# State times weights as 64-column matmuls into the two halves of the output partitions, two tiles per two steps

## The chip, the cores and the metric

The kernel runs on one core of one Trainium2 chip. The metric is the device time of one execution in microseconds (us). A run is timed as a whole; the profile's span, from the first to the last instruction on the core, is a little shorter.

## The reference

`x` is (8, 8, 512, 64): 8 batches, 8 heads, 512 tokens, 64 channels. `state` is (8, 8, 32, 64). Per batch and head:

```
a  = softmax(x @ state.T / 8)   ; xread = a  @ state      (512 x 64)
a2 = softmax(state @ x.T / 8)   ; sread = a2 @ x          ( 32 x 64)
y  = concat of xread and sread over tokens, the heads side by side: (8 * 544, 512)
out = (sigmoid(y @ w_gate) * (y @ w_val)) @ w_out          w_gate, w_val: 512 x 1536, w_out: 1536 x 512
```

## The kernel before

The kernel never forms xread. Since xread of a head is a times that head's state, xread times a weight is a times (state times weight). So for each batch it makes SW, the state of all heads times `w_gate` and `w_val`, and multiplies the attention weights into it. All matmuls are bf16 with fp32 sums in PSUM.

The stationary operand of "state times weight" is `sTz`, filled at L247 to L250. For a pair of heads j it holds 128 columns: the first 64 are the pair's transposed state (head 2j in the upper 64 channel rows, head 2j+1 in the lower, 32 columns each), the last 64 are zeros. `sw_tile(b, t)` (L167 to L179) makes one of the 24 tiles of SW for batch b: 512 columns of one weight (`w` picks gate or value, `q` the third of its columns), and one group `g` of two pairs, whose 2 x 64 rows fill the 128 output partitions. It does so with two matmuls of 128 stationary columns into the whole PSUM tile `swp`, summed up there: the first reads pair 2g with the zeros behind it, so its second 64 output rows get zeros; the second reads the 64 zeros that lie ahead of pair 2g+1, so its first 64 output rows get zeros added. ScalarE then copies the tile to `SW` as bf16 (L179). `swp` has two buffers.

`gv(b, f)` (L182 to L200) makes the gate and the value of 128 of the 1536 columns for 512 tokens: two matmuls each (L192), a tanh on ScalarE (`th`, L199), and a multiply on VectorE (`glu`, L200). `out_mm(b, k)` (L204 to L220) does four matmuls with `w_out` (L209), and every third one is followed by ScalarE's copy of the finished 128x512 tile (`res`, L213) and its DMA; its PSUM pool `p_out` has one buffer, so the next tile's first matmul waits for that copy.

The order is written out by hand in the loop L267 to L310: 12 steps f for each batch b, each with `out_mm` of batch b-1, `gv` of batch b, one `sw_tile` of batch nb = b+1, and then one piece of the attention of batch nb: the transposes of x (`at_xT`, f = 0 and 1), the scores (`at_S`, f = 2 and 3), the normalisation on VectorE (`at_norm`, f = 4 and 5, which makes `ab`), the transposes of `ab` (`at_aT`, f = 6) and sread (`at_sr`, f = 8). In batch 0 the first step of each third of the columns also makes four tiles of SW for batch 0 itself, as the weights arrive by DMA and are cast. In batch 7 there is no next batch, and pass 8 does the sread rows of all batches with plain weights (L195). There is no scheduler: each engine runs its instructions in the order written and waits on semaphores.

Of the kernel before, what the change touches and what calls it, by code (L numbers as in the profile page):

```python
# [16 lines left out]
def kernel(  # L17
# [13 lines left out]
    nc = tc.nc  # L31
# [21 lines left out]
    sTz = wp.tile((128, B, 4, 128), BF, name="sTz")  # L53
# [9 lines left out]
    def load_x(b):  # L63
        xf = stg.tile((128, H, 4, D), FP, name="xf", tag="stg")
        v = x[b].rearrange("h (p c) d -> p h c d", c=4)
        if b == 0:
            for i in range(2):
                nc.sync.dma_start(xf[:, 4 * i:4 * i + 4], v[:, 4 * i:4 * i + 4])
        else:
            nc.sync.dma_start(xf, v)  # L70
        xfs[b] = xf

    def load_w(src, key, q):
        wf = stg.tile((128, 4, 512), FP, name="wf", tag="stg")
        nc.sync.dma_start(wf, src.rearrange("(k p) n -> p k n", p=128)[:, :, q * 512:(q + 1) * 512])
        wfs[key, q] = wf

    def load_wo(q):
        wf = stg.tile((128, 4, 512), FP, name="wof", tag="stg")
        nc.sync.dma_start(wf, moe_w_out.rearrange("(k p) n -> p k n", p=128)[:, 4 * q:4 * q + 4])  # L80
        wfs["o", q] = wf
# [13 lines left out]
    def cast_wo(q):  # L95
        for i in range(4):
            nc.gpsimd.tensor_copy(wo[:, 4 * q + i], wfs["o", q][:, i])


    def at_xT(b, i):  # L100
        if i == 0:
            xTs[b] = ap_.tile((128, 4, 512), BF, name="xT")
        ps = p_at.tile((128, 2, 4, 128), BF, name="xTp", tag="at")
        for jj in range(2):
            for c in range(4):
                j = 2 * i + jj
                nc.tensor.transpose(ps[:, jj, c], xbs[b][:, c, 2 * j:2 * j + 2].rearrange("p h d -> p (h d)"), ident)  # L107
        nc.vector.tensor_copy(xTs[b][:, 2 * i:2 * i + 2], ps.rearrange("p j c t -> p j (c t)"))  # L108

    def at_S(b, i):  # L110
        if i == 0:
            E1s[b] = ap_.tile((128, 4, H * Ns), FP, name="E1")
        ps = p_at.tile((128, 2, H * Ns), FP, name="Sp", tag="at")
        for cc in range(2):
            c = 2 * i + cc
            for j in range(4):
                nc.tensor.matmul(ps[:, cc, j * 64:(j + 1) * 64], xTs[b][:, j, c * 128:(c + 1) * 128],  # L117
                                 sTz[:, b, j, 0:64], start=True, stop=True)
        nc.scalar.activation(E1s[b][:, 2 * i:2 * i + 2], ps, AF.Exp, scale=scale)  # L119

    def at_Eb(b):
        Ebs[b] = ap_.tile((128, 4, H * Ns), BF, name="Eb")
        for c in range(4):
            nc.gpsimd.tensor_copy(Ebs[b][:, c], E1s[b][:, c])  # L124

    def at_norm(b, i):
        if i == 0:
            abs_[b] = ap_.tile((128, 4, H * Ns), BF, name="ab")
        E = E1s[b][:, 2 * i:2 * i + 2].rearrange("p c (h n) -> p (c h) n", n=Ns)
        rs = ap_.tile((128, 16), FP, name="rs")  # L130
        nc.vector.tensor_reduce(rs, E, AX.X, ALU.add)  # L131
        ri = ap_.tile((128, 16), FP, name="ri")
        nc.vector.reciprocal(ri, rs)  # L133
        nc.vector.tensor_tensor(abs_[b][:, 2 * i:2 * i + 2].rearrange("p c (h n) -> p (c h) n", n=Ns), E,  # L134
                                ri.unsqueeze(2).to_broadcast((128, 16, Ns)), ALU.mult)

    def at_aT(b):
        ps = p_at.tile((128, 2, 4, 128), BF, name="aTp", tag="at")
        for g in range(2):
            for c in range(4):  # L140
                nc.tensor.transpose(ps[:, g, c], abs_[b][:, c, g * 128:(g + 1) * 128], ident)  # L141
        aTs[b] = ap_.tile((128, 2, 512), BF, name="aT")
        nc.vector.tensor_copy(aTs[b], ps.rearrange("p g c t -> p g (c t)"))
# [23 lines left out]
    def sw_tile(b, t):  # L167
        if t == 0:
            SWs[b] = fp.tile((128, 2, 2, dff), BF, name="SW", bufs=2)
        q, w, g = t // 4, (t // 2) % 2, t % 2  # L170
        ps = p_sw.tile((128, 512), FP, name="swp")
        W = wg if w == 0 else wv
        for jj in range(2):
            j = 2 * g + jj
            flat = sTz[:, b].rearrange("p j e -> p (j e)")
            lo = j * 128 - 64 * jj
            nc.tensor.matmul(ps, flat[:, lo:lo + 128], W[:, j, q * 512:(q + 1) * 512],  # L177
                             start=(jj == 0), stop=(jj == 1))
        nc.scalar.activation(SWs[b][:, g, w, q * 512:(q + 1) * 512], ps, AF.Copy)  # L179


    def gv(b, f):  # L182
        n = 512 if b < B else B * Ns
        if f == 0:
            glus[b] = fp.tile((128, NF, n), BF, name="glu", bufs=2, padded_shape=(128, NF, 512))
        fs = slice(f * 128, (f + 1) * 128)
        pss = []
        for w in range(2):
            ps = p_gv.tile((128, 512), FP, name="gvp", tag="gv")[:, :n]
            if b < B:  # L190
                for g in range(2):
                    nc.tensor.matmul(ps, SWs[b][:, g, w, fs], aTs[b][:, g], start=(g == 0), stop=(g == 1))  # L192
            else:
                for j in range(4):
                    nc.tensor.matmul(ps, (wg if w == 0 else wv)[:, j, fs], XS[:, j], start=(j == 0), stop=(j == 3))  # L195
            pss.append(ps)
        th = fp.tile((128, 512), FP, name="th")[:, :n]

        nc.scalar.activation(th, pss[0], AF.Tanh, scale=0.5)  # L199
        nc.vector.scalar_tensor_tensor(glus[b][:, f], th, 1.0, pss[1], ALU.add, ALU.mult)  # L200
# [3 lines left out]
    def out_mm(b, k):  # L204
        c, f0 = k // 3, (k % 3) * 4
        if f0 == 0:
            ops[b, c] = p_out.tile((128, 512), FP, name="outp")
        for f in range(f0, f0 + 4):
            nc.tensor.matmul(ops[b, c], glus[b][:, f, c * 128:(c + 1) * 128], wo[:, f],  # L209
                             start=(f == 0), stop=(f == NF - 1))  # L210
        if f0 == 8:
            res = fp.tile((128, 512), FP, name="res")
            nc.scalar.activation(res, ops[b, c], AF.Copy, scale=0.5)  # L213
            if b < B:
                rows = out[b * SC:b * SC + S].rearrange("(p c) n -> c p n", c=4)
                nc.sync.dma_start(rows[c], res)
            else:
                for i in range(4):
                    r0 = (4 * c + i) * SC + S
                    nc.sync.dma_start(out[r0:r0 + Ns], res[i * Ns:(i + 1) * Ns])  # L220
# [20 lines left out]
    for t in range(2):  # L241
        sb = xp.tile((128, H * D), BF, name="sb")
        nc.scalar.activation(sb, sfs[t].rearrange("p h d -> p (h d)"), AF.Copy)  # L243
        ps = p_sw.tile((128, 4, 128), BF, name="stp", tag="swp")
# [22 lines left out]
    for b in range(B + 1):  # L267
        for f in range(NF):
            nb = b + 1 if b + 1 < B else None
            if b == 0:  # L270
                if f % 4 == 0:
                    for t in range(f, f + 4):
                        sw_tile(0, t)
                if f == 1:
                    load_w(moe_w_gate, "g", 2)
                    load_w(moe_w_val, "v", 2)
                if f in (4, 5, 6):
                    load_wo(f - 4)
                if f in (8, 9, 10):
                    cast_wo(f - 8)  # L280
            if b > 0:
                out_mm(b - 1, f)
            gv(b, f)
            if nb is not None:
                sw_tile(nb, f)
                if f == 0:
                    at_xT(nb, 0)
                    if b > 0 and nb + 1 < B:
                        load_x(nb + 1)
                elif f == 1:  # L290
                    at_xT(nb, 1)
                elif f == 2:
                    at_S(nb, 0)
                elif f == 3:
                    at_S(nb, 1)
                elif f == 4:
                    at_norm(nb, 0)
                    at_Eb(nb)
                elif f == 5:
                    at_norm(nb, 1)  # L300
                elif f == 6:
                    at_aT(nb)
                elif f == 8:
                    at_sr(nb)
                if b == 0 and f == 9:
                    load_x(2)
                if nb + 1 < B and f == 11:
                    cast_x(nb + 1, nc.gpsimd, range(4))
            if b == 0 and f in (3, 7):
                cast_w(f // 4 + 1)  # L310
# [32 lines left out]
```

## Time and profile before

| | |
|---|---|
| median of 3 runs | 294.54 us (294.14 to 294.59) |
| the profiled execution's own time | 292.45 us |
| its span | 290.7 us |
| TensorE (PE) busy | 254.0 us, 87% of the span |
| ScalarE (ACT) busy | 152.8 us, 53% |
| VectorE (DVE) busy | 131.7 us, 45% |
| mean granted TensorE clock | 0.998 of 2.4 GHz |

PE is the matrix engine's matmul stream and PEld its weight loads, which lie beside it. A matmul's row has a modelled end, and its duration includes a tail that the next matmul overlaps. So a stream's pace is read from the starts of successive groups, not from durations.

### The profile page before, as it was taken

The page shows a single profiled execution, that of the slowest core. Times are in us where ns is not written, and L with a number is a line of the kernel's source. Part 1 is how long each engine was busy: PE and PEld are TensorE (multiplying, and loading weights), DVE is VectorE, ACT ScalarE, POOL GpSimd, SP SyncE. Part 2 cuts the span into 40 slices and gives each one's busy share as a digit, 9 for nine tenths or more (in the row PEclk, how much of TensorE's full clock was granted, in tenths as well). Part 3 has the DMA queues.
Part 4 walks back from the last instruction along what each step waited for, and adds up shares of the span by engine and source line. Part 5 has one row for each costly group of instructions (what it writes and reads, how often), then busy time and mean ns, then how long its engine had stood idle before and what let it go on. Part 6 is the DMA issues. An engine that isn't in the chain of part 4 may idle for free.

```text
span 290.7 us, 4172 instructions
## 1 busy us (share of the span) xinstructions
PE 254.0 (87%) x1600; PEld 130.8 (45%) x1600; DVE 131.7 (45%) x216; ACT 152.8 (53%) x264; POOL 37.4 (13%) x78
## 2 busy tenths in 40 slices
PE   0044688599999999999999999999999999999993
PEld 0034243245454545454545454545454544456651
DVE  3026364654554455445544554455445543342210
ACT  0333378675755575557555655565566554432330
POOL 0006016800500050005000500050002000000000
PEclk9999999999999999999999999999999999999999
DMA  7977706900110611061105101511101001011102
GB/s 229 338 241 270 293 2 227 341 12 6 53 41 29 177 54 38 28 178 53 39 26 182 48 37 33 183 39 36 38 36 39 36 36 39 36 72 38 72 37 72
DMA packets 20276, 27.53 MB, mean 95 GB/s; under 512 B 3104, under 2 KB 11296, under 8 KB 20256
## 3 DMA queue, kind: packets, MB, share of 16 engines
q1 hardware_dynamic: 18080, 26.74, 27.1%
q10 hardware_dynamic: 2176, 0.52, 0.9%
q8 instruction: 12, 0.20, 0.3%
q14 instruction: 8, 0.07, 0.1%
HBM read 18.35 MB, written 8.91 MB: 94 GB/s over the span
## 4 chain that ended last, share of the span: by engine, by line
PE 77%; DVE 10%; DMA 5%; ACT 4%; issue 1%; ACTq 0%; DVEq 0%
PE outp L209 28%; PE gvp L192 25%; PE swp L177 12%; DMA sf<-in_state_dram 5%; PE gvp L195 4%; PE xTp L107 3%; DVE glu L200 3%; DVE rs L131 3%; DVE ab L134 2%; PE aTp L141 2%; PE srp L157 1%; PE srp L152 1%; ACT wv L93 1%; PE Sp L117 1%; DVE ri L133 1%
## 5 line engine op out<-in xcount | busy, mean ns | idle before, releaser
L200 DVE SCALAR_TENSOR_TENSOR glu<-th,gvp 128x512 bf16<-128x512 f32 (+1 forms) x108 | 70.9, 657 | 124.4 <-ACT th L199 107.4
L209 PE MATMUL outp<-wo,glu 128*128 128x512 bf16 x408 | 104.1, 379 | 0.7 <-ACT res L213 0.7
L192 PE MATMUL gvp<-aT,SW 128*128 128x512 bf16 x384 | 99.7, 382 | 0.1
L199 ACT ACTIVATE th<-gvp 128x512 f32<-128x512 f32 (+1 forms) x108 | 61.7, 572 | 65.5 <-PE gvp L192 55.1
L179 ACT ACTIVATE SW<-swp 128x512 bf16<-128x512 f32 x96 | 56.9, 597 | 30.3 <-PE swp L177 30.3
L192 PEld LDWEIGHTS <-SW 128*128 128x128 bf16 x384 | 37.5, 98 | 45.6 <-ACT SW L179 1.6
L209 PEld LDWEIGHTS <-glu 128*128 128x128 bf16 x408 | 37.9, 98 | 38.0 <-issue 1.0
L124 POOL CAST Eb<-E 128x256 bf16<-128x256 f32 x32 | 13.0, 435 | 179.8 <-ACT E L119 179.8
L177 PE MATMUL swp<-wg,sTz 128*128 128x512 bf16 x96 | 28.9, 389 | 6.4 <-DVE wg L92 6.4
L177 PEld LDWEIGHTS <-sTz 128*128 128x128 bf16 x192 | 19.0, 100 | 31.2 <-issue 6.9
L213 ACT ACTIVATE res<-outp 128x512 f32<-128x512 f32 x34 | 20.3, 597 | 21.0 <-PE outp L209 21.0
L177 PE MATMUL swp<-wv,sTz 128*128 128x512 bf16 x96 | 29.0, 389 | 0.7 <-ACT SW L179 0.7
L108 DVE COPY xT<-xTp 128x1024 bf16<-128x1024 bf16 x16 | 11.1, 691 | 13.8 <-PE xTp L107 13.7
L89 POOL CAST xb<-xf 128x512 bf16<-128x512 f32 x28 | 16.8, 642 | 0.8 <-DMA xf<-in_x_dram 0.8
L246 PE MATMUL stp<-ident,sb 128*128 128x128 bf16 x8 | 1.2, 306 | 16.4 <-ACT sb L243 16.4
L134 DVE TENSOR_TENSOR ab<-E,ri 128x512 bf16<-128x512 f32 x16 | 12.6, 785 | 0.6
L141 PE MATMUL aTp<-ident,ab 128*128 128x128 bf16 x64 | 6.6, 231 | 5.9 <-DVE ab L134 5.2
L107 PE MATMUL xTp<-ident,xb 128*128 128x128 bf16 x128 | 10.6, 230 | 1.1 <-DVE xb L89 1.1
L131 DVE TENSOR_REDUCE rs<-E 128x16 f32<-128x512 f32 x16 | 10.8, 676 | 1.2 <-ACT E L119 1.2
L107 PEld LDWEIGHTS <-xb 128*128 128x128 bf16 x128 | 9.1, 103 | 4.7 <-DVE xb L89 1.4
L119 ACT ACTIVATE E<-Sp 128x512 f32<-128x512 f32 x16 | 9.4, 592 | 3.1 <-PE Sp L117 3.1
L160 DVE RECIPROCAL r<-srp 128x128 f32<-128x128 f32 x8 | 7.7, 957 | 4.0 <-PE srp L157 4.0
(31 smaller groups left out, 102.6 us busy)
## 6 DMA issues: line engine op xcount, KB each, us to landing
out_dram<-res SPq DMA_DIRECT2D x32, 256.0 KB, 2.2
xf<-in_x_dram SPq DMA_DIRECT2D x7, 1024.0 KB, 7.2
wf<-in_moe_w_gate_dram SPq DMA_DIRECT2D x3, 1024.0 KB, 8.3
wf<-in_moe_w_val_dram SPq DMA_DIRECT2D x3, 1024.0 KB, 5.3
wof<-in_moe_w_out_dram SPq DMA_DIRECT2D x3, 1024.0 KB, 5.0
xf<-in_x_dram SPq DMA_DIRECT2D x2, 512.0 KB, 4.8
sf<-in_state_dram ACTq DMA_DIRECT2D x8, 64.0 KB, 8.0
out_dram<-res SPq DMA_DIRECT2D x8, 64.0 KB, 1.7
```

What stands on the lines that cost most here:

```text
L89: eng.tensor_copy(xb.rearrange("p c h d -> p h c d")[:, 2 * i:2 * i + 2], xf[:, 2 * i:2 * i + 2])
L107: nc.tensor.transpose(ps[:, jj, c], xbs[b][:, c, 2 * j:2 * j + 2].rearrange("p h d -> p (h d)"), ident)
L124: nc.gpsimd.tensor_copy(Ebs[b][:, c], E1s[b][:, c])
L131: nc.vector.tensor_reduce(rs, E, AX.X, ALU.add)
L134: nc.vector.tensor_tensor(abs_[b][:, 2 * i:2 * i + 2].rearrange("p c (h n) -> p (c h) n", n=Ns), E, ri.unsqueeze(2).to_broadcast((128, 16, ...
L177: nc.tensor.matmul(ps, flat[:, lo:lo + 128], W[:, j, q * 512:(q + 1) * 512], start=(jj == 0), stop=(jj == 1))
L179: nc.scalar.activation(SWs[b][:, g, w, q * 512:(q + 1) * 512], ps, AF.Copy)
L192: nc.tensor.matmul(ps, SWs[b][:, g, w, fs], aTs[b][:, g], start=(g == 0), stop=(g == 1))
L199: nc.scalar.activation(th, pss[0], AF.Tanh, scale=0.5)
L200: nc.vector.scalar_tensor_tensor(glus[b][:, f], th, 1.0, pss[1], ALU.add, ALU.mult)
L209: nc.tensor.matmul(ops[b, c], glus[b][:, f, c * 128:(c + 1) * 128], wo[:, f], start=(f == 0), stop=(f == NF - 1))
L213: nc.scalar.activation(res, ops[b, c], AF.Copy, scale=0.5)
```

## The change

`sw_tile` no longer pads. Each pair of heads is one matmul with 64 stationary columns, `sTz[:, b, j, 0:64]`, that writes only its own 64 output partitions, and each is a sum of its own. The number of matmuls stays two for each tile, and each still streams 512 columns. In the loop, the tile of an odd step is made in the even step before it, right behind that step's own, so that SW matmuls come four at a time in every second step. The functions around `sw_tile` are unchanged; the lines between it and the loop move up by two (L192 becomes L190).

```diff
         for jj in range(2):
             j = 2 * g + jj
-            flat = sTz[:, b].rearrange("p j e -> p (j e)")
-            lo = j * 128 - 64 * jj
-            nc.tensor.matmul(ps, flat[:, lo:lo + 128], W[:, j, q * 512:(q + 1) * 512],
-                             start=(jj == 0), stop=(jj == 1))
+            nc.tensor.matmul(ps[jj * 64:(jj + 1) * 64], sTz[:, b, j, 0:64], W[:, j, q * 512:(q + 1) * 512],
+                             start=True, stop=True)
         nc.scalar.activation(SWs[b][:, g, w, q * 512:(q + 1) * 512], ps, AF.Copy)
...
             if nb is not None:
-                sw_tile(nb, f)
+                if f % 2 == 0:
+                    sw_tile(nb, f)
+                    sw_tile(nb, f + 1)
                 if f == 0:
```

In the built program each 64-column matmul and its weight load carry the half of the array's columns that they use, the lower for the first pair of a tile and the upper for the second; all 1408 others carry the whole 128 x 128 array. The 192 matmuls of SW stand in 45 groups between the others: 42 of four, and three of eight (batch 0's own tiles).

TensorE before, in batch 1 behind the gate and value matmuls of step f = 4 (`gvp` is their PSUM tile, `sTz` and `glu` name stationary operands):

```order
L192 MATMUL gvp_715<-aT_456,SW_278 128x512
L177 LDWEIGHTS sTz_86
L177 MATMUL swp_721<-wg_87,sTz_86 128x512
L177 LDWEIGHTS sTz_86
L177 MATMUL swp_721<-wg_87,sTz_86 128x512
L209 LDWEIGHTS glu_268
L209 MATMUL outp_680<-wo_89,glu_268 128x512
```

TensorE at the same place in the changed program:

```order
L190 MATMUL gvp_715<-aT_460,SW_278 128x512
L175 LDWEIGHTS sTz_86
L175 MATMUL swp_721<-wg_87,sTz_86 64x512
L175 LDWEIGHTS sTz_86
L175 MATMUL swp_721<-wg_87,sTz_86 64x512
L175 LDWEIGHTS sTz_86
L175 MATMUL swp_725<-wg_87,sTz_86 64x512
L175 LDWEIGHTS sTz_86
L175 MATMUL swp_725<-wg_87,sTz_86 64x512
L207 LDWEIGHTS glu_268
L207 MATMUL outp_684<-wo_89,glu_268 128x512
```

Four half-width matmuls in two PSUM tiles stand where two full-width ones in one tile stood, and step f = 5 has none.

ScalarE before, in batch 1 from the tanh of step 4 on (`res` is the copy that frees the one PSUM buffer of `out_mm`):

```order
L199 ACTIVATE th_718<-gvp_712 128x512
L179 ACTIVATE SW_604<-swp_721 128x512
L213 ACTIVATE res_740<-outp_680 128x512
L199 ACTIVATE th_749<-gvp_743 128x512
L179 ACTIVATE SW_604<-swp_752 128x512
```

ScalarE at the same place in the changed program:

```order
L197 ACTIVATE th_718<-gvp_712 128x512
L177 ACTIVATE SW_604<-swp_721 128x512
L177 ACTIVATE SW_604<-swp_725 128x512
L211 ACTIVATE res_744<-outp_684 128x512
L197 ACTIVATE th_753<-gvp_747 128x512
```

The copy `res` of the odd steps 5 and 11 stands behind two copies of SW instead of one, and the tanh of the odd step follows it.

## Rows read from the trace of the kernel before

**Rows 1.** The page: the span, 40 slices of PE and its clock, chain, weight loads.
```profile
span 290.7 us, 4172 instructions
...
PE   0044688599999999999999999999999999999993
...
PEclk9999999999999999999999999999999999999999
...
PE 77%; DVE 10%; DMA 5%; ACT 4%; issue 1%; ACTq 0%; DVEq 0%
...
L177 PEld LDWEIGHTS <-sTz 128*128 128x128 bf16 x192 | 19.0, 100 | 31.2 <-issue 6.9
```
**Rows 2.** Busy time by stretch: start, batch 0, batches 1 to 6 (span, then engines).
```profile
0.00:41.80 41.80, 17.13 (x126) 10.39 (x127) 15.18 (x27) 14.06 (x21) 5.32 (x14) 1.00 0.71 239
41.80:64.82 23.02, 17.14 (x108) 7.84 (x106) 13.04 (x20) 17.74 (x29) 12.01 (x20) 1.00 0.54 183
64.82:239.12 174.30, 173.57 (x1110) 87.20 (x1109) 90.15 (x145) 104.14 (x181) 20.09 (x44) 1.00 0.19 61
```
**Rows 3.** Timeline of PE, last step of batch 2, first of batch 3: start, us.
```profile
120.54 1.03 PE L209 MATMUL outp<-wo,glu 128*128 128x512 bf16 x4
121.40 1.03 PE L192 MATMUL gvp<-aT,SW 128*128 128x512 bf16 x4
122.27 0.59 PE L177 MATMUL swp<-wv,sTz 128*128 128x512 bf16 x2
122.70 1.03 PE L209 MATMUL outp<-wo,glu 128*128 128x512 bf16 x4
123.56 1.03 PE L192 MATMUL gvp<-aT,SW 128*128 128x512 bf16 x4
124.42 0.59 PE L177 MATMUL swp<-wg,sTz 128*128 128x512 bf16 x2
124.86 0.61 PE L107 MATMUL xTp<-ident,xb 128*128 128x128 bf16 x8
125.30 1.03 PE L209 MATMUL outp<-wo,glu 128*128 128x512 bf16 x4
```
**Rows 4.** Groups of PE by form: busy us, mean ns of one, idle before.
```profile
L209 PE MATMUL outp<-wo,glu 128*128 128x512 bf16 x408 | 104.1, 379 | 0.7 <-ACT res L213 0.7
```
**Rows 5.** Timeline of PE around the transposes of ab in one batch.
```profile
139.58 0.51 PE L141 MATMUL aTp<-ident,ab 128*128 128x128 bf16 x6
...
139.93 0.38 PE L209 MATMUL outp<-wo,glu 128*128 128x512 bf16 x1
```
**Rows 6.** Timeline of all engines, the same batch, from the tanh of step 4.
```profile
133.55 1.03 PE L192 MATMUL gvp<-aT,SW 128*128 128x512 bf16 x4
...
134.81 0.69 DVE L200 SCALAR_TENSOR_TENSOR glu<-th,gvp 128x512 bf16<-128x512 f32 x1 [1.71 <-ACT th L199]
...
138.84 0.69 DVE L134 TENSOR_TENSOR ab<-E,ri 128x512 bf16<-128x512 f32 x1
...
139.16 0.93 PE L141 MATMUL aTp<-ident,ab 128*128 128x128 bf16 x8
```
**Rows 7.** Waits in 64.82 to 239.12 us: total, times, longest.
```profile
PEld L141 <- DVE ab L134: 1.6, 5, 0.3
```
**Rows 8.** Timeline of ACT at the end of batch 2.
```profile
120.74 0.60 ACT L179 ACTIVATE SW<-swp 128x512 bf16<-128x512 f32 x1 [0.27 <-PE swp L177]
121.60 0.60 ACT L213 ACTIVATE res<-outp 128x512 f32<-128x512 f32 x1 [0.27 <-PE outp L209]
```
**Rows 9.** Timeline of PE in the last third of batch 0.
```profile
56.30 1.04 PE L177 MATMUL swp<-wg,sTz 128*128 128x512 bf16 x4 [1.69 <-DVE wg L92]
57.59 1.08 PE L177 MATMUL swp<-wv,sTz 128*128 128x512 bf16 x4 [0.25 <-ACT SW L179]
...
62.23 1.03 PE L192 MATMUL gvp<-aT,SW 128*128 128x512 bf16 x4
63.09 0.59 PE L177 MATMUL swp<-wv,sTz 128*128 128x512 bf16 x2
63.52 1.03 PE L192 MATMUL gvp<-aT,SW 128*128 128x512 bf16 x4
```
**Rows 10.** Timeline of ACT over the same group of four tiles.
```profile
56.95 1.08 ACT L179 ACTIVATE SW<-swp 128x512 bf16<-128x512 f32 x2
58.22 1.08 ACT L179 ACTIVATE SW<-swp 128x512 bf16<-128x512 f32 x2 [0.19 <-PE swp L177]
```

## The prediction

> **What bounds the kernel now.** I read the slices of the page first: from the ninth slice to the last but one PE stands at 9 of 10, at the full clock of 2.4 GHz, and the chain of waits lies on PE for 77% of the span [rows 1]. Then the stretches: in batches 1 to 6, 174.30 us long, PE is busy for 173.57 us, while ACT has 104 us and DVE 90 us of work; in batch 0 PE has 17 us of 23 and ACT 17.7 us [rows 2]. So a change on PE is worth its full size in batches 1 to 6 and little before. Last the pace. In the timeline of PE four matmuls of 512 columns take 121.40 - 120.54 = 0.864 us and the two of an SW tile 122.70 - 122.27 = 0.432 us: 0.216 us each, with no gap between groups, whatever the operands [rows 3]. One matmul's row is 0.379 us long [rows 4], so a tail of 0.163 us lies beside its successor. Weight loads of 0.100 us each for SW [rows 1] lie beside running matmuls as well, and eight transposes follow each other in 125.30 - 124.86 = 0.44 us, 0.055 us each, a new weight load for each [rows 3].
>
> **The change part by part.** The number of matmuls, their columns and the copies to SW stay. What is new is that a matmul holds half of the array's columns and writes half of the partitions, and that its partner has the other half: other weights, another right-hand side, other output rows.
>
> *1. Two halves at once.* No row of this trace has two matmuls in two parts of the array, so the price of a pair is bounded: from above by two in turn, 0.432 us; from below by one behind which the second starts as soon as its weights are in, 0.216 + 0.055 = 0.271 us. I take the lower end, since the two share neither columns nor outputs, and since loading weights beside a running matmul is what the rows show all the time. A group of four (two pairs) then holds PE for 0.432 + 0.055 = 0.487 us, where its four matmuls took 0.864 us: 0.377 us gained. There are 6 x 6 = 36 such groups in batches 1 to 6: 13.6 us.
>
> The Trainium skill speaks for the lower end ("TensorE: Matmul & The Clock Gate", section "Measured speedup vs the span model"): three matmuls in separate column strips ran 2.38 times as fast as in turn. No run here shows it yet; by the other bound of the pair part 1 would be worth nothing.
>
> *2. The switches.* Each group is entered from full-width matmuls and left to them. What one such switch costs (call it s) no row shows. From below: nothing, as transposes, scores and 512-column matmuls follow each other without a gap [rows 3]. From above: if the array has to be empty first, the tail of 0.163 us and then a weight load that could not run ahead, 0.100 us [rows 1], together 0.26 us. The nearest row is PE's restart after the wait for `ab`: six transposes from 139.58 to 139.93, 0.35 us against 6 x 0.055 = 0.33 us [rows 5], so a late weight load itself cost about 0.02 us there, and an empty array would cost 0.18 us. Whether the array has to be empty is open, so I take the middle of the two bounds, s = 0.13 us. Per group 2 x 0.13 = 0.26 us is given back, and 0.117 us is left; over 36 groups 4.2 us. The group pays for itself up to s = 0.19 us.
>
> *3. The transposes of `ab`.* From the tanh of step 4 VectorE works without a pause, from 134.81 until `ab` is done at 138.84 + 0.69 = 139.53 [rows 6], and PE waits 0.3 us for it in the middle of the transposes, five times [rows 7]. The work of VectorE does not change. On PE, between the first half of step 4's `gv` and the transposes, stand 24 matmuls now, 24 x 0.216 = 5.19 us; after the change two, a group of four, sixteen, a group of four: 18 x 0.216 + 2 x 0.487 + 4s = 4.86 + 4s. At s = 0.13 that is 5.38 us, 0.19 us more slack, so the waits shrink from 0.3 to 0.1 us: 5 x 0.19 = 0.9 us gained. At s = 0 they grow by 0.33 us in each of six batches, 2.0 us; at 0.26 they are gone, 1.6 us gained.
>
> *4. ScalarE behind a pair of tiles.* Copies of SW now come two in a row, and in steps 5 and 11 the copy `res`, on which the next `out_mm` waits for its only PSUM buffer, stands behind both. From the rows a copy starts about 0.42 us after its last matmul starts and lasts 0.60 us, and `res` starts 0.20 us after PE leaves `out_mm` [rows 3, 8]. Counted from the first half-width matmul: the two copies run from 0.475 to 1.675 us, `res` could start at 0.487 + s + 0.864 + 0.20 = 1.55 + s, and PE asks for the buffer at 0.487 + s + 1.728 = 2.215 + s. With `res` from 1.68 to 2.28 us and 0.05 us to signal, PE waits 0.11 - s: nothing at s = 0.13, and at s = 0 twelve times 0.11, 1.3 us. A tanh behind the copies has over 1.2 us until its buffer is needed. The tile that is made a step earlier is used only in the next batch, its PSUM buffer is the other of two, and the next group comes over 3.9 us later. No DMA, no instruction of POOL or VectorE moves.
>
> *5. Batch 0.* The three groups of eight wait for weights and then go at ScalarE's pace: four copies from 56.95 to 59.30 us, 0.59 us each, against 0.43 us of PE for a tile [rows 9, 10], so neither a faster pair nor a switch shows: 0. The six groups of four stand in steps of 63.52 - 62.23 = 1.29 us on PE against two copies, 1.18 us, on ScalarE [rows 9, 10]: two steps can gain 0.2 us at most, and at s = 0.26 they lose 0.14 us each. I take 0, with bounds of 0.5 us gained and 0.9 us lost. Batch 7 and pass 8 have no SW.
>
> **Sum.** -4.2 (parts 1 and 2) - 0.9 (part 3) + 0 + 0 = -5.1 us. The profiled execution, 292.45 us (290.7 in the span and 1.75 around it), becomes 287.3 us. It lies 2.1 us under the median of the runs shown; against that median of 294.54 us the forecast is **289.4 us**. At s = 0 with the full gain it is -13.6 + 2.0 + 1.3 = -10.3 us, 284.2 us, and 1 or 2 us less if the second half starts at once and batch 0 gives its bit.
>
> **Rivals.**
>
> *The array must be empty at every switch.* Then s is 0.18 to 0.26 us, and from 0.19 us on the group loses: at 0.26 us 36 x 0.143 = 5.1 us, and 0.9 us in batch 0, less the 1.6 us of the vanished waits: +4.4 us, 298.9 us. It decides from s = 0.21 us on, where 42 groups x (0.42 - 0.377) = 1.8 us outweigh the 1.6 us of the vanished waits. For it speaks that the restart row prices it at 0.18 us even with a cheap weight load; against it that no change of shape in the rows opens a gap. The Trainium skill states this rule ("TensorEngine Tiling (Array Packing)", section "Key Properties"): changing the tiling mode drains the engine. The trace before has one mode only and can't agree or disagree.
>
> *The halves run one after the other* (the change does not do what it is for). Then nothing is gained and only switches are paid: 42 groups x 2s less the vanished waits. At s = 0.13 that is 42 x 0.26 - 1.6 = +9.3 us, 303.9 us; at 0.05 it is about +3.5 us, 298 us; at s = 0 no change. For it speaks that no row shows two matmuls at once, against it that they share no column.
>
> *The overlap is full and switches are nearly free.* Then VectorE's `ab` and ScalarE's `res` are what PE waits for next, and the time is the 284.2 us worked out above.
>
> **How the numbers follow.** About 0.2% of the median, 0.6 us, is what a measurement can tell from no change. The halves overlap and s is under 0.20: 0.58, of which the free switch is about 0.18; this is "faster", and its own range is 282.5 to 293.5 us. They overlap and s is above 0.21: 0.17. They run in turn and switches cost: 0.15, so "slower" is 0.32. The narrow strip around s = 0.21, or halves in turn with free switches, makes "same" 0.10. The range for 8 in 10 takes in both ends of s with overlap, 283 to 299, and the cheaper part of the third case, up to 301 us.
>
> **What would show it.** In the profile after, the two matmuls of a pair should start about 0.06 us apart, and from the point where the full-width stream would go on to the next full-width matmul a group of four should take 0.487 + 0.26 = 0.75 us, where four took 0.864. A start 0.216 us after its partner's shows halves in turn; 0.9 us or more for a group shows the empty array. PE's wait for `ab` should fall to about 0.1 us, with no wait for `res` in batches 1 to 6. A granted clock below 1.00 in batches 1 to 6, or a wait of PE for `swp`, would make the sum wrong in a way that it does not count.

## The result and the profile after

The changed kernel takes 286.36 us (median of 4 runs, 285.03 to 287.04) against 294.48 us: a ratio of 0.9721, interval 0.9685 to 0.9757. A second series gave 286.36 us and 0.9732 (0.9700 to 0.9765). That is 8.1 us faster, where 5.1 us were forecast, inside the stated range. The profiled execution is one at the median: 286.36 us, span 284.6 us. The profiled execution of before was 2 us faster than its median, so the two spans differ by 6.1 us only.

The page after, with the lines that answer to [rows 1]:

```profile
span 284.6 us, 4172 instructions
...
PE   0034596499999999999999999999999999999993
...
PEclk9999997979999999999999999999999999999999
...
PE 77%; DVE 10%; DMA 5%; ACT 4%; issue 2%; ACTq 0%
...
L175 PEld LDWEIGHTS <-sTz 128*64 128x64 bf16 x192 | 7.9, 112 | 30.7 <-issue 25.3
```

PE bounds the kernel as before. What is new is the clock's line: in the seventh and the ninth slice, both in batch 0, the granted clock is below 1.00.

Busy time by stretch, answering to [rows 2]: start, batch 0, batches 1 to 6 up to the same matmul of batch 7 (span, then PE, PEld, DVE, ACT, POOL, clock, DMA share, GB/s).

```profile
0.00:41.65 41.65, 16.62 (x129) 9.77 (x130) 15.10 (x27) 14.06 (x22) 5.33 (x14) 1.00 0.74 240
41.65:65.89 24.24, 17.10 (x106) 6.30 (x105) 13.25 (x20) 17.58 (x29) 12.34 (x20) 0.86 0.51 174
65.89:233.03 167.14, 166.26 (x1110) 75.21 (x1109) 88.90 (x145) 100.91 (x182) 20.17 (x44) 1.00 0.19 62
```

Batches 1 to 6 lost 174.30 - 167.14 = 7.2 us. Batch 0 ended 1.1 us later, at a mean clock of 0.86. The timeline of PE in the changed kernel, answering to [rows 3]:

```profile
122.18 1.03 PE L190 MATMUL gvp<-aT,SW 128*128 128x512 bf16 x4
123.13 0.62 PE L175 MATMUL swp<-wg,sTz 128*64 128x512 bf16 x4
123.69 0.62 PE L107 MATMUL xTp<-ident,xb 128*128 128x128 bf16 x8
124.14 1.03 PE L207 MATMUL outp<-wo,glu 128*128 128x512 bf16 x4
```

The four `gv` matmuls from 122.18 on hold PE for 0.864 us, to 123.04. The group of four starts at 123.13, so the switch in costs 0.09 us, and the next full-width matmul starts at 123.69: from 123.04 the group held PE for 0.65 us, where its four matmuls took 0.864. All 36 groups of batches 1 to 6 hold it for 0.65 us. A closer look inside the group (the first two matmuls alone, and the weight loads):

```profile
123.13 0.41 PE L175 MATMUL swp<-wg,sTz 128*64 128x512 bf16 x2
```
```profile
123.13 0.14 PEld L175 LDWEIGHTS <-sTz 128*64 128x64 bf16 x4 [0.42 <-issue]
```

The rows of the first two matmuls last 0.403 us each and the two together 0.41 us, so both start within 0.01 us of each other: the halves run at once. All four weight loads lie in the group's first 0.14 us, none ahead of it. The Trainium skill ("TensorE: Matmul & The Clock Gate", section "Measured speedup vs the span model") gives about 4 ns from one packed matmul to the next, and the trace agrees within that hundredth.

### The profile page after: what moved, and what is told of

It is laid out like the page before. It is cut to its first block, busy times and chain, and to the rows that moved or that the text cites. A ratio compares the mean times of both kernels' runs of the same rounds, so it can differ in the third digit from the quotient of the medians.

```text
span 284.6 us, 4172 instructions
## 1 busy us (share of the span) xinstructions
PE 246.2 (87%) x1600; PEld 116.6 (41%) x1600; DVE 130.8 (46%) x216; ACT 149.4 (53%) x264; POOL 37.8 (13%) x78
## 4 chain that ended last, share of the span: by engine, by line
PE 77%; DVE 10%; DMA 5%; ACT 4%; issue 2%; ACTq 0%
PE outp L207 30%; PE gvp L190 25%; PE swp L175 9%; DMA sf<-in_state_dram 5%; PE gvp L193 4%; PE xTp L107 3%; DVE glu L198 2%; DVE ab L134 2%; DVE rs L131 2%; ACT th L197 2%; PE srp L152 2%; PE aTp L141 2%; PE Sp L117 2%; PE srp L157 1%; DVE wg L92 1%
## 5 line engine op out<-in xcount | busy, mean ns | idle before, releaser
L190 PE MATMUL gvp<-aT,SW 128*128 128x512 bf16 x384 | 100.5, 385 | 0.1
L177 ACT ACTIVATE SW<-swp 128x512 bf16<-128x512 f32 x96 | 52.1, 594 | 17.5 <-PE swp L175 16.1
L190 PEld LDWEIGHTS <-SW 128*128 128x128 bf16 x384 | 37.2, 99 | 46.2 <-issue 2.5
L207 PEld LDWEIGHTS <-glu 128*128 128x128 bf16 x408 | 37.0, 98 | 40.1 <-issue 5.9
L175 PE MATMUL swp<-wg,sTz 128*64 128x512 bf16 x96 | 16.5, 427 | 7.6 <-DVE wg L92 7.6
L175 PEld LDWEIGHTS <-sTz 128*64 128x64 bf16 x192 | 7.9, 112 | 30.7 <-issue 25.3
L108 DVE COPY xT<-xTp 128x1024 bf16<-128x1024 bf16 x16 | 11.0, 688 | 15.4 <-PE xTp L107 15.4
L175 PE MATMUL swp<-wv,sTz 128*64 128x512 bf16 x96 | 16.5, 418 | 1.0 <-ACT SW L177 1.0
L134 DVE TENSOR_TENSOR ab<-E,ri 128x512 bf16<-128x512 f32 x16 | 11.6, 727 | 0.6
```

The lines of the kernel that those rows point to most:

```text
L175: nc.tensor.matmul(ps[jj * 64:(jj + 1) * 64], sTz[:, b, j, 0:64], W[:, j, q * 512:(q + 1) * 512], start=True, stop=True)
```

## The experiments

**Two halves at once, or something else in the edit?** The edit does three things together: narrower weight loads, two halves of the array, and groups of two tiles. The first three runs take them apart.

*One tile in every step, halves as in the change.*

```diff
-                if f % 2 == 0:
-                    sw_tile(nb, f)
-                    sw_tile(nb, f + 1)
+                sw_tile(nb, f)
```

> Halves as in the change, but one tile in every step: 12 groups of two matmuls in a batch where the change has 6 of four. If the gain is two halves at once, less about 0.19 us for the two switches of a group (0.085 us in, 0.10 us out in the profile after), a group of two holds PE for 0.216 + 0.03 + 0.19 = 0.43 us, what two full-width matmuls held it for: batches 1 to 6 take 173 us as before, and the time is 293 to 295 us. If the gain came from narrower weight loads or from the padding that is gone, it does not depend on the grouping, and the time stays at 286 us.

Measured: 292.72 us, ratio 0.9968 (0.9935 to 1.0002). Its timeline of PE:

```profile
117.50 0.59 PE L190 MATMUL gvp<-aT,SW 128*128 128x512 bf16 x2
118.03 0.41 PE L175 MATMUL swp<-wg,sTz 128*64 128x512 bf16 x2
118.36 1.04 PE L207 MATMUL outp<-wo,glu 128*128 128x512 bf16 x4
119.24 0.59 PE L190 MATMUL gvp<-aT,SW 128*128 128x512 bf16 x2
```

From 117.50 + 0.432 = 117.93, where the full-width stream ends, to 118.36 a group of two holds PE for 0.43 us, as two full-width matmuls did. The two switches eat the overlap, as expected (the time came out just under the 293 to 295 us forecast): from batch 1's first matmul to batch 7's PE needs 173.6 us, before it was 173.4 and in the change 166.3. The gain depends on the grouping, so narrow weight loads or the missing padding alone do not bring it.

*The grouping alone, with the padded full-width matmuls of before.*

```diff
-                sw_tile(nb, f)
+                if f % 2 == 0:
+                    sw_tile(nb, f)
+                    sw_tile(nb, f + 1)
```

> Full-width padded matmuls as before, but two tiles in every second step: the grouping alone. Halves at once: no gain, 294 to 295 us, batches 1 to 6 at 173 to 175 us. If the grouping brings the gain, by fewer waits between PE and ScalarE: 286 to 288 us. Its batch 0 tells whether the 1.1 us that batch 0 lost come with the grouping (it ends 1 us late here too) or with the halves (it ends as before, near 64.8 us, at a granted clock of 1.00).

Measured: 293.53 us, ratio 0.9992 (0.9962 to 1.0022): the grouping alone brings nothing that can be told from no change. In its profiled execution batch 0 ended at 66.6 us, 1.8 us late, with padded matmuls throughout. So batch 0 can end late without the halves. Whether the grouping makes it late is taken up below.

*Both matmuls of a tile in the lower half.*

```diff
-            nc.tensor.matmul(ps[jj * 64:(jj + 1) * 64], sTz[:, b, j, 0:64], ...
+            nc.tensor.matmul(ps[0:64], sTz[:, b, j, 0:64], ...
-        nc.scalar.activation(SWs[b][:, g, w, q * 512:(q + 1) * 512], ps, AF.Copy)
+        nc.scalar.activation(SWs[b][0:64, g, w, q * 512:(q + 1) * 512], ps[0:64], AF.Copy)
```

> The change with both 64-column matmuls of a tile in the lower half of the columns and of the output partitions; the upper half of SW is set to zero by POOL, so half of the heads are left out. Same number of matmuls, same narrow weight loads, same grouping and switches, but no second half to run beside. If the gain is two at once, a group takes four matmuls in turn, 4 x 0.216 + 0.19 = 1.05 us instead of 0.65: 36 x 0.40 = 14 us more than the change, about 300 us, 6 us slower than before. If the gain lies in the narrow loads, 286 us.

Measured: 304.60 us, ratio 1.039 (1.0336 to 1.0444). Its timeline of PE:

```profile
118.14 1.05 PE L176 MATMUL swp<-wv,sTz 128*64 128x512 bf16 x4
119.12 0.62 PE L141 MATMUL aTp<-ident,ab 128*128 128x128 bf16 x8
```

The same four narrow matmuls with the same narrow loads now take 0.98 us from their start instead of 0.56, about what four in turn would. From the start of batch 1 to the matmul behind the last group this kernel needs 178.0 us and the change 164.5: 13.5 us, the 14 us expected. By the groups alone it would be 15.4 us: from the end of the full-width stream each holds PE for 1.08 us instead of 0.65, 36 times. The other 1.9 us come back because the transposes of `ab` no longer wait here as they do in the change: the eight in the last line above take 0.46 us to the next matmul, in the change 0.78. The whole time is 4 to 5 us above the 300 us expected because batch 0 was late as well, by 5.5 us more than in the change; its own memsets on POOL and its longer groups lie there, and it was not taken apart. The gain is shown to be the overlap of two halves.

**Does the order in the queue matter?** The two lower halves of a group first, then the two upper ones (the two tiles' copies follow both):

```diff
+        pss = [p_sw.tile((128, 512), FP, name="swp") for _ in range(2)]
+        for jj in range(2):
+            for g in range(2):
+                j = 2 * g + jj
+                nc.tensor.matmul(pss[g][jj * 64:(jj + 1) * 64], sTz[:, b, j, 0:64], W[:, j, q * 512:(q + 1) * 512],
+                                 start=True, stop=True)
```

> The change with one thing else: within a group the two tiles' lower halves are issued first, then the two upper halves, so that neighbours in the queue want the same half. If matmuls start in the order of the queue and two run at once only when neighbours want different halves, a group takes one matmul more, 0.216 us x 36 = 7.8 us: 294 us. If a matmul may start before its turn when its half is free, or if the gain is not the overlap at all: 286 us.

Measured: 286.53 us, ratio 0.974 (0.9687 to 0.9792), as the change. The first expectation is wrong. The group of this kernel:

```profile
120.06 0.41 PE L189 MATMUL swp<-wv,sTz 128*64 128x512 bf16 x2
```
```profile
120.06 0.62 PE L189 MATMUL swp<-wv,sTz 128*64 128x512 bf16 x4
```

Two start together and four take 0.62 us, as in the change, though the second in the queue wants the same half as the first. With the run before, where matmuls of one half went in turn, this means that an upper half's matmul starts ahead of a lower half's that stands in front of it. The semaphores in the trace's single records say the same: a lower half's matmul waits for its PSUM tile and an upper half's signals that the tile is done, and in all 36 groups the four start in the order waits, signals, waits, signals, where the queue has waits, waits, signals, signals. Matmuls are not started strictly in the order of the queue across halves.

**Batch 0 and the clock.** In the changed kernel batch 0 by stretches of the granted clock, and its longest wait:

```profile
44.40:47.80 3.40, 2.95 (x10) 0.90 (x11) 0.13 (x1) 2.55 (x5) 2.63 (x5) 0.50 0.45 152
47.80:58.00 10.20, 5.91 (x35) 2.09 (x34) 7.75 (x12) 6.86 (x11) 6.57 (x11) 1.00 1.02 347
58.00:61.50 3.50, 3.46 (x12) 0.87 (x11) 0.40 (x1) 2.16 (x4) 1.04 (x2) 0.51 0.12 41
```
```profile
44.59 1.06 PE L175 MATMUL swp<-wg,sTz 128*64 128x512 bf16 x4 [2.54 <-DVE wg L92]
```

Twice the clock is at 1.2 GHz for 3.4 us; ahead of the first, PE had stood idle for 2.54 us, waiting for cast weights, and in the stretch ahead of the second it was busy for 5.9 us of 10.2. The first trial put batch 0 back to what it was:

```diff
+            if full:
+                flat = sTz[:, b].rearrange("p j e -> p (j e)")
+                lo = j * 128 - 64 * jj
+                nc.tensor.matmul(ps, flat[:, lo:lo + 128], W[:, j, q * 512:(q + 1) * 512],
+                                 start=(jj == 0), stop=(jj == 1))
+                continue
...
-                        sw_tile(0, t)
+                        sw_tile(0, t, True)
...
+                if b == 0:
+                    sw_tile(nb, f, True)
-                if f % 2 == 0:
+                elif f % 2 == 0:
```

> Batch 0 with full-width matmuls, one tile in each step, as before; halves in groups of four from batch 1 on. If the halves and their grouping cost batch 0 its 1.1 us, by longer idle of PE after which the granted clock falls to 1.2 GHz for a while, then batch 0 ends near 64.8 us again with the clock at 1.00, batches 1 to 6 take 166 us, and the time is 1 to 1.5 us under that of the change, 285 us. If batch 0's millimetres come from the DMA of that run alone, no difference, 286 us.

(The last sentence of the expectation speaks of batch 0's 1.1 us.) Measured: 287.03 us, ratio 0.9765 (0.9726 to 0.9805), no better than the change. Its batch 0 ended at 67.4 us although its instructions are those of before. Its stretches show 10.2 us at 1.2 GHz, where the profiled execution of before had none [rows 2]:

```profile
44.80:48.20 3.40, 3.27 (x8) 1.10 (x8) 0.00 (x0) 2.27 (x5) 1.44 (x3) 0.51 0.84 302
48.20:55.10 6.90, 4.71 (x27) 2.23 (x27) 6.29 (x10) 3.23 (x7) 5.55 (x9) 0.99 1.01 346
55.10:61.90 6.80, 5.32 (x13) 1.52 (x12) 1.95 (x2) 5.07 (x8) 3.21 (x4) 0.50 0.33 108
```

The expectation falls: batch 0 ends late, and the clock falls in it, without the edit too. The same batch 0 gets a fallen clock in one execution and none in another. Nor does every fall show in the time: the run with one tile in every step had 3.4 us at 1.2 GHz too, from 57.0 to 60.4 us, and ended batch 0 at 64.8 us like before. Over whole executions time and clock go together: in one series of 23 of the kernel before, those with a mean clock of 0.997 or 0.998 took 291.9 to 293.1 us, those at 0.985 or below 294.3 to 295.5 us. The next trial goes for the idle time itself, eight extra matmuls ahead of the second and the third group of batch 0's own tiles:

```diff
+            nc.tensor.matmul(dum[0], ones[:, 0], wg[:, 0, 0:512], start=True, stop=True)
...
+                    if f > 0:
+                        keep_busy(8)
```

> The change with eight extra full-width matmuls (1.7 us, into a PSUM tile that nobody reads) ahead of the second and third group of batch 0's own tiles, where PE waits for weights 2.5 and 2.1 us. If the granted clock falls in batch 0 because PE sits idle there, it stays at 1.00 up to batch 7 in most executions, batch 0 ends 1 to 2 us earlier, and the time is 284.5 to 285.5 us with less spread. If the clock has other reasons, or costs nothing because ScalarE sets the pace there, 286 to 287 us.

Measured: 284.18 us (283.22 to 284.81), ratio 0.9682 (0.9649 to 0.9715), with mean clocks of 0.991 to 1.00, where the change itself had 0.979 to 0.992 in its ten executions, in other series. Batch 0 ended at 64.3 us in the profiled execution, though that one still had one stretch of 3.4 us at 1.2 GHz:

```profile
51.86 0.51 PE L141 MATMUL aTp<-ident,ab 128*128 128x128 bf16 x6 [1.76 <-DVE ab L134]
52.21 1.62 PE L190 MATMUL gvp<-aT,SW 128*128 128x512 bf16 x4
53.62 3.03 PE L227 MATMUL outp<-wg,ones 128*128 128x512 bf16 x8
```

The wait for `ab`, 1.76 us, was not filled, and the clock fell behind it (the eight extra matmuls then took 3.0 us instead of 1.7). The next two versions, which were timed beside this one, have no extra matmuls in batch 0: their mean clocks were 0.982 to 0.994, so the higher clock goes with the filling. But their profiled executions ended batch 0 at 64.1 and 63.7 us, as early as this one, and the interval of the ratio overlaps that of the change (0.9685 to 0.9757). So that the filling makes batch 0 shorter is not shown. Whether the edit makes a fall likelier than before is not settled either: the kernel before was also seen at 0.983.

**More from fewer switches.** Groups of three tiles need a third PSUM buffer for SW, which the attention's pool gives up:

```diff
-    p_sw = ctx.enter_context(tc.tile_pool(name="p_sw", bufs=2, ...
-    p_at = ctx.enter_context(tc.tile_pool(name="p_at", bufs=2, ...
+    p_sw = ctx.enter_context(tc.tile_pool(name="p_sw", bufs=3, ...
+    p_at = ctx.enter_context(tc.tile_pool(name="p_at", bufs=1, ...
...
+                k = 2 if b == 0 else 3
+                if f % k == 0:
+                    for t in range(f, f + k):
+                        sw_tile(nb, t)
```

> The change with groups of three tiles (six matmuls) in every third step from batch 1 on: four groups a batch instead of six. It takes a third PSUM buffer for SW from the attention's pool, which keeps one. If a group's fixed price is 0.19 us of switches, and each further pair 0.216 us, a group of three takes 0.19 + 0.03 + 3 x 0.216 = 0.87 us, where twelve tiles took 6 x 0.65 = 3.9 us and now take 4 x 0.87 = 3.5: 6 x 0.4 = 2.5 us gained, 284 us. But only one group stands between step 4 and the transposes of ab, so PE's wait for VectorE there grows by about 0.4 us in each batch and gives the gain back: 286 us. A start stage that grows by the single attention buffer would show ahead of batch 0.

Measured: 284.06 us, ratio 0.9694 (0.9654 to 0.9734); from batch 1's first matmul to batch 7's it needs 165.4 us, 0.9 us less than the change. Most of the rest of the 2.5 us went where it was expected, into the wait for `ab`, as its table of waits in batches 1 to 6 shows:

```profile
PEld L141 <- DVE ab L134: 3.7, 6, 0.6
PE aTp L141 <- DVE ab L134: 2.7, 6, 0.5
```

The weight loads of these transposes waited 3.7 us here and 1.9 us in the change (its row stands further below). The time is nevertheless at the 284 us of the full gain, because batch 0 ended at 64.1 us in the profiled execution, 1.8 us ahead of the change; the start stage did not grow, and why batch 0 was shorter was not taken apart. So the transposes of `ab` were moved one step later:

```diff
-                elif f == 6:
+                elif f == 7:
                     at_aT(nb)
```

> As the groups of three, with the transposes of ab one step later (step 7), so that VectorE has about 1.7 us more. If the wait for ab is what gives the gain back, it is gone now, its 0.3 us of before too: 6 x 0.7 = 4 us under the groups of three alone, 282 to 283 us. If PE waits somewhere else (for res or a PSUM buffer), less.

Measured: 279.54 us (279.13 to 279.72), ratio 0.9533 (0.9503 to 0.9564). The expectation had 4 us under the groups of three alone, and it is 4.5; the 282 to 283 us it gave were counted from 286. In batches 1 to 6 no wait of PE or of its weight loads names `ab` any more, and from batch 1's first matmul to batch 7's it needs 161.6 us, 4.7 us less than in the change and 11.8 us less than before. A group of three in its timeline, with the four `gv` matmuls ahead of it:

```profile
118.45 1.03 PE L190 MATMUL gvp<-aT,SW 128*128 128x512 bf16 x4
119.41 0.62 PE L175 MATMUL swp<-wg,sTz 128*64 128x512 bf16 x4
119.87 0.38 PE L175 MATMUL swp<-wv,sTz 128*64 128x512 bf16 x2
120.18 0.62 PE L107 MATMUL xTp<-ident,xb 128*128 128x128 bf16 x8
```

Six matmuls hold PE from 118.45 + 0.864 = 119.31 to 120.18: 0.87 us, as worked out, where six in turn take 1.296. Then both gains together, with no further edit:

> Groups of three tiles, the transposes of ab in step 7, and the eight extra matmuls twice in batch 0. If the two gains lie in different stretches (batches 1 to 6: 4.6 us against the change; batch 0: about 1.5 us) they add: 1 to 2 us under the groups of three with the later transposes, 0.947 to 0.950 of before. If batch 0's gain is lost to the wait for ab's transposes or to the clock falling elsewhere, 0.953 as without it.

Measured: 278.89 us (277.62 to 279.44), ratio 0.9475 (0.9439 to 0.9511), clocks of 0.997 to 0.999 in all six executions. Batches 1 to 6 again need 161.6 us, and batch 0 ended at 63.2 us with no fall of the clock. It is the fastest version here by its median, 5% under before and 2.6% under the change, which was timed beside it. The ratio is the one expected, but its interval touches that of the version without the extra matmuls (0.9503 to 0.9564), so what they add is not told apart with certainty. The change:

> The change itself, on the same chip and in the same rounds as the version above, to place both against one series of before. Batches 1 to 6 should take 166 us again whatever batch 0 does, and the ratio should be 0.972 to 0.977; the spread of a few us should go with the granted clock of each execution.

Measured: 286.36 us, ratio 0.9732, as quoted above, with clocks of 0.979 to 0.986 where the version above had 0.997 to 0.999.

## Why the prediction was right

*What bounds.* Right: all of the gain in the compared profiles lies in batches 1 to 6, at PE's pace.

*Part 1, two halves at once.* Right, shown by the rows of the group and by the run with one half. The lag of the second half was put at 0.055 us; the two start within 0.01 us, and the second pair follows the first by 0.24 us (0.62 us for four, 0.38 for the last alone), so a group of four loses 0.024 us where 0.055 was counted.

*Part 2, the switches.* The mechanism was right, the term was mis-sized. A switch was put at 0.13 us, the middle of 0 and 0.26 us. It costs 0.09 us in and 0.10 us out (0.56 us from the group's start to the next full-width matmul, less 0.24 and 0.216). A group holds PE for 0.65 us instead of 0.75, which is 0.214 us gained instead of 0.117: 36 x 0.214 = 7.7 us instead of 4.2. These 3.5 us are more than the 3.0 us between the forecast of 5.1 and the 8.1 measured; part 3 took some of them back.

*The rival of the empty array.* The Trainium skill's rule that a change of mode drains the engine ("TensorEngine Tiling (Array Packing)", section "Key Properties") fits a price of this kind, and a kernel with a group in every step gains nothing that can be told apart from zero. But the price stays under the 0.163 us of the tail alone, so the sum by a full drain, 298.9 us, did not come. The row on which that end rested has a modelled end; it bounds the price and does not measure it. What the 0.09 and 0.10 us consist of stays open: they are near the 0.11 us of a half-width weight load's row, and the group's loads do not run ahead of it, but no run takes the two apart.

*Part 3, the transposes of `ab`.* The bound was right, the sign of the chosen value was not: with s at 0.09 to 0.10 and the smaller lag, PE's way between the two points is 18 x 0.216 + 2 x 0.65 = 5.19 us, exactly the 5.19 us of before, so the waits stayed, and grew by 0.3 us in all, instead of shrinking by 0.9 us. In the changed kernel's waits in batches 1 to 6, answering to [rows 7]:

```profile
PEld L141 <- DVE ab L134: 1.9, 6, 0.3
```

Before, this row had 1.6 us. The 7.7 us of part 2 less these 0.3 us make 7.4 us, and the profiles show 7.2 us in batches 1 to 6. The 0.9 us by which the medians differ beyond that were not taken apart.

*Part 4, ScalarE.* Right: in the changed kernel's timeline of ACT the copy `res` of step 5 follows the two copies of SW directly and PE does not wait for it.

```profile
133.16 1.09 ACT L177 ACTIVATE SW<-swp 128x512 bf16<-128x512 f32 x2 [0.17 <-PE swp L175]
134.35 0.60 ACT L211 ACTIVATE res<-outp 128x512 f32<-128x512 f32 x1
```

*Part 5, batch 0.* Nothing was expected there, and the profiled executions differ by 1.1 us against the change. The prediction named a granted clock below 1.00 as something that the sum does not count, but only for batches 1 to 6; it fell in batch 0. The execution of before shown in the rows had no such fall, so they gave no sign of it.

*The halves in turn* is excluded by the group's 0.65 us, where the run with one half, which does go in turn, has 1.08. That this run's 304.6 us lie near the 303.9 us of this rival is chance: in its profiled execution 6.3 us more than before lie between the first matmuls of batches 1 and 7, and 6.6 us lie ahead of them, for which the rival's sum has nothing.

## What to carry to other kernels

Padding a stationary operand with zeros to fill the array cost full matmul time here, 0.43 us for a pair; two half-width matmuls into the two halves of the output partitions did the same work in about half of it, 0.22 to 0.24 us. The change of width has a fixed price, here 0.19 us for both ways, close to one 512-column matmul: a group of two gains nothing, a group of four 25% of its time, a group of six a third, which took a third PSUM buffer. After such a gain, look for the chain that was just hidden (here VectorE's softmax in front of a transpose) and move its consumer; here that was worth 3.7 us, and the larger groups alone 0.9 us.

## What was not expected of the hardware

Across the two halves, matmuls do not start in the order of the queue: with lower, lower, upper, upper in the queue, an upper one started together with the first lower one, and the time was that of the alternating order (286.53 against 286.36 us). That each engine runs its instructions in the order written, as the section on the kernel before has it, is so for the queue and not for these starts. And the granted clock differs from one execution to the next of the same kernel: a mean of 0.983 to 0.998 for the kernel before, with which about 2.5 us go (292.3 us at 0.997, 295.0 at 0.985). From batch 0 on, the falls in the profiled executions lie in batch 0 and in the last few us.
